# A spectral layer and a gated layer on one core: the forward transform along time over two row groups, and a later start of four inverse tiles

## The chip, the cores and the metric

The kernel runs on one core of one Trainium2 chip. The core has five engines that work side by side, each on its own queue of instructions: TensorE (PE in the profile, with PEld for its weight loads), VectorE (DVE), ScalarE (ACT), GpSimd (POOL) and SyncE (SP), which here issues most transfers. Matrix products land in PSUM, which has eight banks of 128 x 512 numbers of four bytes here; everything else lies in SBUF, and large arrays come from the device's memory by DMA.

The metric is the device time of one execution in microseconds (us), as the median of several runs.

## The reference: what is computed

The input x has 2048 rows (time) of 512 numbers. Four residual layers follow each other; two kinds alternate:

```
x = x + A(layernorm(x));  x = x + B(layernorm(x));  x = x + A(layernorm(x));  x = x + B(layernorm(x))

A(x) = irfft2(rfft2(x) * (w_r + 1j * w_i))          # spectral filter, transform over both axes
B(x) = ((x @ w_gate) * (x @ w_up)) @ w_down         # 512 -> 1792 -> 512, no nonlinearity
```

So each spectral layer is a two-dimensional real Fourier transform, a product with a complex filter of 2048 x 257 numbers, and the inverse transform. Each gated layer is three matrix products. Both layers of a kind use the same weights.

## The kernel before, in words

**Data.** x stays in SBUF all the time as `xs`, 16 tiles of 128 rows by 512. A tile holds 2 x 64 of the 2048 rows. The transform along time is split as 64 points within a tile and 32 across tiles.

**Forward transform** (`fwd_steps`, lines 211 to 283), four steps per tile. `a0`: sums and differences of the halves of a row (fo, fe, on POOL and DVE) and the load of the tile's table `tw`. `a1`: four transposes on TensorE into a bank tp, copied to fs by ACT or DVE; the last argument of `fwd_steps`, `fs_dve`, says for which tiles DVE does it. `a2`: the transform along the 512 features, four matmuls into a bank dp; then dp is scaled by the norm's factor into `us`. dp has real parts (257 columns) and imaginary parts (255 columns) side by side, and rows of two groups of 64; `us` has to put the imaginary parts of a group below its real parts, so four ACT instructions of 64 rows move the four quarters, and POOL clears the two columns that have no imaginary part. `a3`: the transform along time within the tile, for each of two groups one matmul of 128 rows by 257 columns into a bank sp, copied by ACT into E. The steps of one tile stand at steps n, n+1, n+2 and n+4 of a list, so that tiles overlap.

**Middle** (`mid_phase`): transposes, the 32-point transform across tiles, the product with the filter, and back into E.

**Inverse transform** (`inv_steps`, lines 377 to 431). For each tile: `b0` loads its table, `b1` is the transform within the tile (vp, split into a high part vs[0] by ACT and a low part vs[1] by DVE), `b2` the transform along the features (yi, 12 matmuls), `b3` and `b4` add the result to xs, and then come the statistics of the next norm: `stats`, `rstd` and `rest`.

**Preparing the gated layer** (`build_x`, lines 433 to 489). Tiles come in pairs (t, t+4). `norm` makes two normed tiles xn (DVE), `turn` transposes one of them on TensorE into a bank tq, and `forms` makes the sums that the products need: copies into `sx` (ACT), four sums (POOL), and splits into high and low parts: XA (ACT, DVE) and XS (ACT, then POOL). `sx` has one buffer. For the second half of x, `sums` takes the place of `forms`, with a stage tile xf.

**Gated layer** (`unit`, lines 554 to 642). The 1792 hidden features are 14 blocks; a unit is one block with 512 or 256 columns of x. It has seven products (p5, p1, p6, p2, p7, p3, p4; gw, gx, gy, gx, gz, gv, gz in the profile), whose factors on the weights' side are made by ACT and POOL (`forms_w`: wt, rg). Two halves of h follow, split into high and low by ACT and POOL, and the products `down` (db), which DVE adds into xs, are handed on to the next unit.

**Order of the work.** The list of `in_steps` is sorted by step and then by a rank. `weave(main, side, frac)` (line 650) mixes two lists by costs that stand in them: after each entry of the main list, entries of the side list are taken as long as their share of the side's cost is behind the main's share of `frac` times its cost. After entries marked "hold" (the last two products of a unit) none is taken, and what is left comes at the end. While `pin["on"]` is set, each engine keeps the order in which the kernel issues its instructions; outside (forward stage of layer 0, its counterpart at the end of layer 0, middle and first part of the inverse) a scheduler may order them by what is ready.

**Where these lists stand.** In each of two rounds (`layer`): middle; the inverse of the first eight tiles (`o1`: 0, 4, 1, 5, 2, 6, 3, 7), of which the entries below step 9 are issued at once and the rest woven into the units (0, 0) and (1, 0), block 0 and 1 on the first 256 columns; then (0, 1) and (1, 1) on the other 256 columns; then blocks 2 to 12, into which the inverse of the other eight tiles and their `norm`, `turn` and `sums` are woven; then the units of the second half of x. At the end of the first round the forward transform for the second is woven in: tiles 0 to 7 while blocks 11 to 2 run, and 8 to 15 at the last units and after them.

All engine instructions are issued through one helper, so the profile shows line 123 for all of them; groups are told apart by the names of their tiles.

Of the kernel before, what the change touches and what calls it, by code (L numbers as in the profile page):

```python
# [33 lines left out]
def consts():  # L34
    odd = np.arange(1, 256, 2)
    ev2 = np.arange(2, 256, 4)
    ev0 = np.arange(0, 256, 4)
    kd = np.concatenate([ev0, ev2, odd, [256]])
    d2 = np.arange(128)[:, None]
    c, s = _cs(d2 * odd[None], 512)  # L40
    sg = np.where(odd % 4 == 1, 1.0, -1.0)[None]
    fb = np.concatenate([c, -s], 1)
    fe = np.concatenate([-s * sg, -c * sg], 1)
    c, s = _cs(d2 * ev0[None], 512)
    nyq = np.where(d2 % 2 == 0, 1.0, -1.0)
    ui = -s
    ui[:, 0:1] = nyq
    fu = np.concatenate([c, ui], 1)
    c, s = _cs(d2 * ev2[None], 512)
    fv = np.concatenate([c, -s], 1)  # L50
    dfwd = np.concatenate([fb, fe, fu, fv], 1)
    d = np.arange(256)[None]
    blocks = []
    ev = np.concatenate([ev0, ev2])[:, None]
    for ks in (ev, odd[:, None]):
        c, s = _cs(ks * d, 512)
        re, im = 2 * c / 512, -2 * s / 512
# [24 lines left out]
    mid = np.concatenate([f2, g2, np.eye(128)], 1).astype(np.float32)  # L82
    single = lambda a: a.astype(np.float32)
    return dict(kd=kd, dfwd=single(dfwd), dinv=np.stack(_split(dinv), 1), tf=single(m), ti=single(r), mid=mid)


@with_exitstack
def kernel(ctx: ExitStack, tc: tile.TileContext, x, wf, wc, wb, dfwd, dinv, tf, ti, mid, out):
# [7 lines left out]
    XYW = "xyw"  # L96
# [114 lines left out]
    def fwd_steps(get_dc, E, tags, gs, fs_dve):  # L211
# [31 lines left out]
        def a2(t):  # L243
            s, dc = S[t], get_dc()
            fs = s["fs"]
            dp = bank("dp", tags(t)[1])
            dv = dp.rearrange("p (c k) -> p c k", c=2)
            o = 0
            for i, (n, c0) in enumerate(((256, 128), (256, 128), (128, 0), (128, 64))):
                mv = dc[:, o:o + n].rearrange("p (c k) -> p c k", c=2)  # L250
                TE.matmul(dv[:, :, c0:c0 + n // 2], fs[:, 128 * i:128 * i + 128], mv,
                                 start=i == 0, stop=i == 3, skip_group_check=True)
                o += n
            u = s["u"] = temp("us", "g", (128, 2, 257))
            G.memset(u[64:128, :, 0:257:256], 0.0)
            i = nms[t]["ts"].index(t)
            r = nms[t]["r"][:, i:i + 1]
            for jj in range(2):
                q = slice(64 * jj, 64 * jj + 64)
                A.mul(u[0:64, jj, 0:257], dp[q, 0:257], r[q])  # L260
                A.mul(u[64:128, jj, 1:256], dp[q, 257:512], r[q])

        def a3(t):
            s = S[t]
            tw, u = s["tw"], s["u"]
            for jj in range(2):
                sp = bank("sp", tags(t)[2])
                TE.matmul(sp[:, :257], tw[:, jj], u[:, jj, 0:257], start=True, stop=True)
                A.copy(E[:, t, :, jj], sp[:, 0:257])
            s.clear()  # L270

        ops = []
# [101 lines left out]
            if i == 8:  # L374
                dcs["i"] = load_di()

    def inv_steps(E, get_dc, nms, order, tags, build):
        S = [{} for _ in range(16)]

        def b0(t):  # L380
# [38 lines left out]
        ops = []  # L419
        for n, t in enumerate(order):  # L420
            nm = nms[t]
            for d, f, o, c in ((0, b0, 3, 0), (1, b1, 2, 1.0), (2, b2, 4, 1.42), (2, b3, 5, 0.3), (2, b4, 6, 0.3)):
                ops.append((n + d, o, c, lambda f=f, t=t: f(t)))
            ops.append((n + 2, 7, 0.3, lambda t=t: stats(t, nms[t])))
            if t == nm["ts"][-1]:
                ops.append((n + 2, 8, 0, lambda nm=nm: rstd(nm)))
                ops.append((n + 3, 3, 0.1, lambda nm=nm: nm["rest"]()))
            if build and n % 2:
                for k, (c, f) in enumerate(build(nm)):
                    ops.append((n + 4 + k // 2, 9, c, f))  # L430
        return in_steps(ops)

    def build_x(X, nm, tags, stage=None):
# [229 lines left out]
    dcs = {}  # L663
# [8 lines left out]
    for n, o in enumerate(fwd_steps(lambda: dcs["f"], E, lambda t: (XYW[t % 3], "a", "d"), G0, lambda t: t % 2)):  # L672
        o[-1]()
        if n >= 40 and n % 2 and pre:
            for f in pre.pop(0):
                f()
        if n in (30, 38, 46, 54, 62):
            W.load((0, 1, 2, 4, 5)[(n - 30) // 8], E[0:1, n // 8 - 3, 0, 0:1])
    prep_hp(E[0:1, 10, 0, 0:1])

    for layer in range(2):
# [61 lines left out]
        if layer == 0:  # L743
            early = lambda t: "aaa"
            late = lambda t: (XYW[t % 3], "a", "d")
            K = 7
            fb = fwd_steps(lambda: dcs["f"], E, early, [(8, 9), (12, 13)], lambda t: t % 2)
            fc = [(o[0] + K, *o[1:]) for o in fwd_steps(lambda: dcs["f"], E, late, [(10, 11), (14, 15)], lambda t: t % 2)]
            weave(ops, [o for o in fb if o[0] < K])
            W = Filter()  # L750
            for m in range(3):
# [52 lines left out]
```

## Time and profile before

| | us |
|---|---|
| median of 3 runs | 1271.33 |
| lowest, highest run | 1269.25, 1273.46 |
| time of the profiled execution | 1267.3 |
| its span | 1265.5 |
| TensorE busy in it | 1146.9 (91%) |
| POOL busy | 749.7 (59%) |
| DVE busy | 880.9 (70%) |
| ACT busy | 461.6 (36%) |

The page of the profile gives, for one execution, the busy time of each engine, a strip of 40 slices of the span with a digit for each (tenths of the slice that the engine was busy), and groups of instructions as `out<-in` by tile names with a count and a mean time. Answers from the trace add: busy time by windows of time, where after the window's bounds and length come PE, PEld, DVE, ACT and POOL, each with the number of instructions in brackets, then the granted clock of TensorE, the share of the DMA engines and GB/s; the timeline (start, length, engine, instruction, and in square brackets the idle time before it and what ended it); the chain of work that ended last (start, length, engine and tile); and waits (who waited for whom: us in total, times, longest). A row of a tile gives the shortest, median and longest time of one instruction in ns, then the first and last start. Matmuls on fp32 data are recorded as two passes each, so that four matmuls are eight rows.

### The profile page before, as it was taken

The numbers are of one execution on the slowest core, as the hardware profiler recorded it, in microseconds if no ns is written. First come the engines' busy times: TensorE is split into PE (matmuls) and PEld (weight loads), VectorE is DVE, ScalarE is ACT, GpSimd is POOL, SyncE is SP. The second block draws the span as 40 slices with busy tenths as digits, with TensorE's granted clock in tenths as the row PEclk, the third lists the DMA queues.
The fourth block names the chain that finished last, engine by engine and source line by source line (L and its number), as shares of the span: only waits on it lengthen the run. The fifth ranks groups of instructions, "written<-read, shape, count | busy, mean of one in ns | idle before, by whom it ended". The sixth has DMA issues, their size and how long they took to land.

```text
span 1265.5 us, 16593 instructions
## 1 busy us (share of the span) xinstructions
PE 1146.9 (91%) x5804; PEld 943.0 (75%) x5804; DVE 880.9 (70%) x1661; ACT 461.6 (36%) x939; POOL 749.7 (59%) x812
## 2 busy tenths in 40 slices
PE   5889669999998999999988885799998989999998
PEld 4645558888777877888877365688887779788887
DVE  7558756777775887775676886566677767666676
ACT  5776223222233233444326742232232332322221
POOL 4534347666676477775741433576666855877772
PEclk9899889999998999999989997899999999999999
DMA  6532001111210011112105310021110210211111
GB/s 234 196 125 67 20 15 51 51 46 51 67 59 26 1 43 47 46 51 75 42 18 220 113 47 22 1 71 38 50 58 24 79 59 34 67 59 51 34 35 67
DMA packets 30755, 77.68 MB, mean 61 GB/s; under 512 B 3408, under 2 KB 11856, under 8 KB 28368
## 3 DMA queue, kind: packets, MB, share of 16 engines
q1 hardware_dynamic: 29952, 73.54, 17.3%
q0 software_dynamic: 288, 2.10, 0.5%
q8 instruction: 46, 0.75, 0.2%
q10 hardware_dynamic: 432, 0.98, 0.2%
q14 instruction: 37, 0.30, 0.1%
HBM read 72.42 MB, written 4.19 MB: 61 GB/s over the span
## 4 chain that ended last, share of the span: by engine, by line
PE 35%; POOL 14%; issue 6%; DVE 5%; ACT 2%; DMA 1%; POOLq 0%; DVEq 0%; ACTq 0%
PE db L123 11%; PE gz L123 5%; PE gx L123 5%; POOL wt L123 5%; POOL rg L123 3%; PE gw L123 3%; PE gy L123 3%; PE gv L123 3%; POOL h L123 2%; PE dp L123 2%; DVE xs L123 1%; DVE q L123 1%; POOL jz L123 1%; PE sp L123 1%; PE yi L123 1%
## 5 line engine op out<-in xcount | busy, mean ns | idle before, releaser
L123 PE MATMUL db<-wd,h 128*128 128x512 f32 x1344 | 367.5, 399 | 10.2 <-ACT h L123 4.0
L123 DVE TENSOR_TENSOR xs<-xs,db 128x512 f32<-128x512 f32 x448 | 297.0, 681 | 49.0 <-PE db L123 48.8
L123 POOL TENSOR_TENSOR h<-q,h 128x512 fp32r<-128x512 f32 (+1 forms) x144 | 151.6, 1057 | 251.4 <-ACT h L123 169.4
L123 PEld LDWEIGHTS db<-wd,h 128*128 128x128 f32 x1344 | 244.5, 191 | 62.6 <-DVE xs L123 9.3
L123 POOL TENSOR_TENSOR wt<-rg,wt 128x512 fp32r<-128x512 f32 (+1 forms) x216 | 233.8, 1090 | 68.9 <-ACT wt L123 67.4
L123 ACT CAST h<-q 128x512 fp32r<-128x512 f32 (+1 forms) x144 | 75.4, 525 | 330.1 <-DVE q L123 310.8
L123 PE MATMUL gx<-xA,wt 128*128 128x512 f32 (+1 forms) x864 | 185.0, 351 | 2.7 <-ACT s L123 2.7
L123 ACT CAST wt<-rg 128x512 fp32r<-128x512 f32 (+1 forms) x216 | 110.6, 541 | 190.3 <-POOL rg L123 176.2
L123 DVE TENSOR_TENSOR q<-gy,s 128x512 f32<-128x512 f32 (+1 forms) x72 | 41.1, 571 | 177.4 <-ACT wt L123 73.2
L123 PEld LDWEIGHTS gx<-xA,wt 128*128 128x128 f32 x864 | 144.7, 196 | 23.8 <-ACT s L123 4.6
L123 POOL TENSOR_TENSOR rg<-rg 128x256 f32<-128x256 f32 x200 | 149.0, 745 | 10.9
L123 PE MATMUL gw<-xS,wt 128*128 128x512 f32 (+1 forms) x432 | 94.8, 354 | 32.1 <-ACT xS L123 22.2
L123 PEld LDWEIGHTS gw<-xS,wt 128*128 128x128 f32 x432 | 72.4, 196 | 45.2 <-ACT xS L123 23.2
L123 PE MATMUL gy<-xS,wt 128*128 128x512 f32 (+1 forms) x432 | 93.7, 354 | 2.0 <-ACT wt L123 1.4
L123 PE MATMUL gz<-xS,wt 128*128 128x512 f32 (+1 forms) x432 | 90.5, 345 | 0.0
L123 PE MATMUL gv<-xS,wt 128*128 128x512 f32 (+1 forms) x432 | 89.7, 343 | 0.0
L123 PE MATMUL gz<-xA,wt 128*128 128x512 f32 (+1 forms) x432 | 89.0, 341 | 0.0
L123 PEld LDWEIGHTS gy<-xS,wt 128*128 128x128 f32 x432 | 73.0, 199 | 12.0 <-ACT wt L123 1.8
L123 PEld LDWEIGHTS gz<-xS,wt 128*128 128x128 f32 x432 | 72.5, 190 | 12.3
L123 PEld LDWEIGHTS gz<-xA,wt 128*128 128x128 f32 x432 | 72.1, 188 | 12.0
L123 PEld LDWEIGHTS gv<-xS,wt 128*128 128x128 f32 x432 | 71.9, 188 | 12.0
L123 ACT ACTIVATE us<-dp,rs 64x257 f32<-64x257 f32 (+1 forms) x128 | 60.3, 471 | 36.2 <-PE dp L123 29.9
(94 smaller groups left out, 1585.8 us busy)
## 6 DMA issues: line engine op xcount, KB each, us to landing
rg<-in_wb_dram SPq DMA_DIRECT2D x50, 512.0 KB, 3.5
rw<-in_wb_dram SPq DMA_DIRECT2D x52, 256.0 KB, 2.6
wq<-in_wf_dram SPq DMA_DIRECT2D x10, 1024.0 KB, 5.8
wr<-in_wf_dram SPq DMA_DIRECT2D x6, 1024.0 KB, 5.7
tw<-in_tf_dram SPq DMA_DIRECT2D x32, 128.0 KB, 2.4
tw<-in_ti_dram SPq DMA_DIRECT2D x32, 128.0 KB, 2.1
out_dram<-xs SPq DMA_DIRECT2D x16, 256.0 KB, 2.0
xs<-in_x_dram SPq DMA_DIRECT2D x7, 512.0 KB, 7.9
```

Of the source, the lines that this page charges most:

```text
L123: ins = f(*args, **kw)
```

## The change

It has three parts.

1. Forward transform. `us` becomes a plain tile of 128 x 512, written by one scaling of the whole of dp; the clearing on POOL goes. The table `tf` is laid out anew, so that each group of 64 rows of `us` finds its table in the same rows. In `a3` each group's product is two matmuls of 64 rows, over the 257 real and over the 255 imaginary columns, added up in PSUM; the two groups use rows 0 to 63 and 64 to 127, and alternate. Both sp banks are taken before the first matmul. `fs_dve` is false everywhere, so that ACT makes all fs copies.
2. Inverse transform, first eight tiles. Tiles 2, 6, 3 and 7 stand two steps later in the list, with all that follows from them. The weave into the first two units uses 0.95 where it used 0.8.
3. Main weave. The norms of a pair are issued one pair ahead of its transposes.

```diff
-    return dict(..., tf=single(m), ti=single(r), mid=mid)
+    return dict(..., tf=single(m.reshape(2, 64, 16, 2, 128).transpose(3, 1, 2, 0, 4).reshape(128, 32, 128)), ti=single(r), mid=mid)
...
-            u = s["u"] = temp("us", "g", (128, 2, 257))
-            G.memset(u[64:128, :, 0:257:256], 0.0)
+            u = s["u"] = temp("us", "g")
             i = nms[t]["ts"].index(t)
-            r = nms[t]["r"][:, i:i + 1]
-            for jj in range(2):
-                q = slice(64 * jj, 64 * jj + 64)
-                A.mul(u[0:64, jj, 0:257], dp[q, 0:257], r[q])
-                A.mul(u[64:128, jj, 1:256], dp[q, 257:512], r[q])
+            A.mul(u, dp, nms[t]["r"][:, i:i + 1])
 
         def a3(t):
             s = S[t]
             tw, u = s["tw"], s["u"]
+            sp = [bank("sp", tags(t)[2]) for _ in range(2)]
+            for c, (lo, n) in enumerate(((0, 257), (1, 255))):
+                for jj in range(2):
+                    q = slice(64 * jj, 64 * jj + 64)
+                    TE.matmul(sp[jj][:, lo:lo + n], tw[q, c], u[q, 256 * c + lo:256 * c + lo + n],
+                              start=c == 0, stop=c == 1, skip_group_check=True)
             for jj in range(2):
-                sp = bank("sp", tags(t)[2])
-                TE.matmul(sp[:, :257], tw[:, jj], u[:, jj, 0:257], start=True, stop=True)
-                A.copy(E[:, t, :, jj], sp[:, 0:257])
+                A.copy(E[:, t, :, jj], sp[jj][:, 0:257])
...
-    def inv_steps(E, get_dc, nms, order, tags, build):
+    def inv_steps(E, get_dc, nms, order, tags, build, late=()):
...
+            m = n + 2 if t in late else n
             for d, f, o, c in ((0, b0, 3, 0), (1, b1, 2, 1.0), (2, b2, 4, 1.42), (2, b3, 5, 0.3), (2, b4, 6, 0.3)):
-                ops.append((n + d, o, c, lambda f=f, t=t: f(t)))
+                ops.append((m + d, o, c, lambda f=f, t=t: f(t)))
...
-    for n, o in enumerate(fwd_steps(..., lambda t: t % 2)):
+    for n, o in enumerate(fwd_steps(..., lambda t: False)):
...
-                         lambda nm: build_x(X, nm, ("d", "d") if nm["ts"][0] < 2 else ("a", "a")))
+                         lambda nm: build_x(X, nm, ("d", "d") if nm["ts"][0] < 2 else ("a", "a")), (2, 6, 3, 7))
...
-        weave(units([(0, 0), (1, 0)], 0), rest, 0.8)
+        weave(units([(0, 0), (1, 0)], 0), rest, 0.95)
...
-        weave(main, inv2 + [o for pre, _ in both for o in pre], 0.93)
+        pre = [p for p, _ in both]
+        early = [pre[0][0]]
+        for k in range(4):
+            early += [pre[k + 1][0]] if k < 3 else []
+            early += pre[k][1:]
+        weave(main, inv2 + early, 0.93)
...
-            fb = fwd_steps(lambda: dcs["f"], E, early, [(8, 9), (12, 13)], lambda t: t % 2)
+            fb = fwd_steps(lambda: dcs["f"], E, early, [(8, 9), (12, 13)], lambda t: False)
```

The same step m takes the place of n for `stats`, `rstd`, `rest` and the build of a pair, and the list `fc` of the last four forward tiles loses its DVE copies like `fb`.

More of the change, by code (lines that the diff above doesn't have):

```diff
@@ L83, in consts @@
     single = lambda a: a.astype(np.float32)
-    return dict(kd=kd, dfwd=single(dfwd), dinv=np.stack(_split(dinv), 1), tf=single(m), ti=single(r), mid=mid)
+    return dict(kd=kd, dfwd=single(dfwd), dinv=np.stack(_split(dinv), 1), tf=single(m.reshape(2, 64, 16, 2, 128).transpose(3, 1, 2, 0, 4).reshape(128, 32, 128)), ti=single(r), mid=mid)
 @with_exitstack
@@ L421, in inv_steps @@
             nm = nms[t]
+            m = n + 2 if t in late else n
             for d, f, o, c in ((0, b0, 3, 0), (1, b1, 2, 1.0), (2, b2, 4, 1.42), (2, b3, 5, 0.3), (2, b4, 6, 0.3)):
-                ops.append((n + d, o, c, lambda f=f, t=t: f(t)))
-            ops.append((n + 2, 7, 0.3, lambda t=t: stats(t, nms[t])))
+                ops.append((m + d, o, c, lambda f=f, t=t: f(t)))
+            ops.append((m + 2, 7, 0.3, lambda t=t: stats(t, nms[t])))
             if t == nm["ts"][-1]:
-                ops.append((n + 2, 8, 0, lambda nm=nm: rstd(nm)))
-                ops.append((n + 3, 3, 0.1, lambda nm=nm: nm["rest"]()))
+                ops.append((m + 2, 8, 0, lambda nm=nm: rstd(nm)))
+                ops.append((m + 3, 3, 0.1, lambda nm=nm: nm["rest"]()))
             if build and n % 2:
                 for k, (c, f) in enumerate(build(nm)):
-                    ops.append((n + 4 + k // 2, 9, c, f))
+                    ops.append((m + 4 + k // 2, 9, c, f))
         return in_steps(ops)
@@ L671 @@
         pre += [[f[k] for k in g.split()] for g in ("start h0", "h12 l0", "d0", "l12", "d1", "d2", "d3 h34", "h56 l34", "l56 next")]
-    for n, o in enumerate(fwd_steps(lambda: dcs["f"], E, lambda t: (XYW[t % 3], "a", "d"), G0, lambda t: t % 2)):
+    for n, o in enumerate(fwd_steps(lambda: dcs["f"], E, lambda t: (XYW[t % 3], "a", "d"), G0, lambda t: False)):
         o[-1]()
@@ L746 @@
             K = 7
-            fb = fwd_steps(lambda: dcs["f"], E, early, [(8, 9), (12, 13)], lambda t: t % 2)
-            fc = [(o[0] + K, *o[1:]) for o in fwd_steps(lambda: dcs["f"], E, late, [(10, 11), (14, 15)], lambda t: t % 2)]
+            fb = fwd_steps(lambda: dcs["f"], E, early, [(8, 9), (12, 13)], lambda t: False)
+            fc = [(o[0] + K, *o[1:]) for o in fwd_steps(lambda: dcs["f"], E, late, [(10, 11), (14, 15)], lambda t: False)]
             weave(ops, [o for o in fb if o[0] < K])
```

## The prediction

> **What bounds the kernel now.** I read the page first (shares, then the strip of 40 slices), then the busy time by windows of 20 us, then the stretch at each change with windows cut at its own events, and last the waits and the timeline there.
>
> ```profile
> span 1265.5 us, 16593 instructions
> ## 1 busy us (share of the span) xinstructions
> PE 1146.9 (91%) x5804; PEld 943.0 (75%) x5804; DVE 880.9 (70%) x1661; ACT 461.6 (36%) x939; POOL 749.7 (59%) x812
> ...
> PE   5889669999998999999988885799998989999998
> ```
>
> TensorE is 91% busy, so the kernel as a whole is bound by it; but the strip (slices of 31.6 us, counted from 0) has three kinds of places that are not nines: slices 0 to 2 and 20 to 23 (forward transforms and what follows), 4 and 5 with 24 and 25 (inverse transforms and the first units), and the eights of 12, 30 and 32 (end of the main weave and the units behind it). The change works at just these.
>
> ```profile
> core 0: us, PE busy (x) PEld busy (x) DVE busy (x) ACT busy (x) POOL busy (x), PEclk, DMA share, GB/s
> 40.00:60.00 20.00, 14.45 (x79) 12.25 (x78) 9.05 (x23) 16.35 (x39) 11.87 (x17) 0.92 0.35 124
> 600.00:620.00 20.00, 20.00 (x90) 16.56 (x89) 12.42 (x20) 6.74 (x14) 15.51 (x17) 1.00 0.13 40
> 680.00:700.00 20.00, 15.37 (x77) 11.61 (x75) 8.12 (x31) 15.18 (x36) 2.12 (x7) 0.91 0.65 254
> ```
>
> In the forward stages (40 to 60 and 680 to 700) ACT is the busiest engine, with TensorE close behind. Where forward tiles are woven into the gated layer (600 to 620) TensorE is full: every matmul added there is added to the time. The third place, by windows cut at the events of layer 0:
>
> ```profile
> core 0: us, PE busy (x) PEld busy (x) DVE busy (x) ACT busy (x) POOL busy (x), PEclk, DMA share, GB/s
> 140.00:148.20 8.20, 1.52 (x10) 1.11 (x10) 7.98 (x18) 3.55 (x7) 3.59 (x5) 0.84 0.00 1
> 148.20:150.65 2.45, 0.58 (x2) 0.29 (x2) 0.07 (x1) 0.00 (x0) 2.34 (x1) 0.50 0.00 0
> 150.65:173.20 22.55, 18.77 (x123) 17.52 (x123) 12.01 (x28) 4.84 (x10) 6.73 (x7) 0.89 0.09 24
> 173.20:181.44 8.24, 0.61 (x3) 0.29 (x2) 3.13 (x7) 3.50 (x7) 5.60 (x7) 0.69 0.00 0
> ```
>
> From 140 to 181.4 us TensorE loses 8.5 us before the first units, 3.8 us inside them, and 7.6 us before the third unit. No engine is full in the last of these: it is a chain of dependent work.
>
> **The change, part 1: forward transform.** Per tile it removes four ACT scalings of 64 rows, and puts one of 128x512 in their place; removes a small POOL memset; moves twelve copies fs of odd tiles from DVE to ACT; and turns two matmuls of 128 rows by 257 columns into four of 64 rows by 257 or 255 columns.
>
> ```profile
> L123 ACT ACTIVATE us<-dp,rs x128: 457/472/476, 14.5 to 695.5; 64x257 f32<-64x257 f32 x64, 64x255 f32<-64x255 f32 x64
> L123 ACT COPY fs<-tp x20: 567/587/605, 10.9 to 688.4; 128x512 f32<-128x512 f32 x20
> L123 DVE COPY fs<-tp x12: 670/680/692, 13.6 to 689.6; 128x512 f32<-128x512 f32 x12
> L123 PE MATMUL sp<-us,tw x128: 377/380/794, 20.5 to 698.6; 128*128 128x257 f32 x128
> L123 ACT COPY E<-sp x64: 380/391/402, 22.4 to 699.0; 128x257 f32<-128x257 f32 x64
> ```
>
> ACT per tile now: 4 x 0.472 + 2 x 0.391 = 2.67 us, and 0.587 more for even tiles: 2.96 on the mean. After: 0.59 (estimate from the fs copy, same shape and source) + 0.78 + 0.59 = 1.96. ACT gives up 1.0 us per tile, DVE 0.68 on odd tiles.
>
> TensorE per tile, from the chain of layer 1, and the pace at which tiles pass in layer 0 (the second fence, from the timeline: with 44.62 and 47.30 between them, three tiles in 9.07 us, 3.0 us each):
>
> ```profile
> 688.15 0.99 PE sp L123 x4
> 689.14 0.44 PE tp L123 x4
> 689.58 2.62 PE dp L123 x16
> 692.20 0.87 PE sp L123 x4
> 693.07 2.47 issue
> ```
>
> ```profile
> 41.31 1.11 PE L123 MATMUL sp<-us,tw 128*128 128x257 f32 x4 [0.16 <-issue]
> ...
> 50.38 1.11 PE L123 MATMUL sp<-us,tw 128*128 128x257 f32 x4 [0.26 <-issue]
> ```
>
> 0.44 + 1.31 + 0.87 = 2.62 us per tile. Each matmul is recorded as two passes, 0.217 us apart. What four half-height matmuls cost no row shows: the nearest is sp itself. Low end: the halves run side by side at all times, eight passes in the time of four, 0.87 us, nothing added. High end: one after another, 1.74 us. In the order of issue (group 0 twice, group 64 twice, and again) only passes next to each other in different groups can overlap, three pairs of eight passes, which leaves five steps: 1.09 us, +0.22. If TensorE must also run empty between full-height and half-height work, each of two changes per tile shows at most the part of a pass that is hidden today, 0.380 - 0.217 = 0.16. I take +0.35 per tile; ends 0 and 0.87 + 0.33 = +1.2. The accumulation also lets the first E copy start only after the third matmul, some 0.5 us later; two banks are free for it, so nothing waits.
>
> The Trainium skill, TensorEngine Tiling (Array Packing), Key Properties, says that different tiles execute in parallel but that a change of tiling mode drains TensorE. No run here shows either. By the first clause alone part 1 would be free on TensorE in the woven tiles; by the second the two changes per tile come on top, and the rival without overlap below is what is left if the first does not hold for this order of issue.
>
> Layer 0's forward stage: the pace goes from 3.0 (ACT) to 2.62 + 0.35 = 2.97 (TensorE), so the pace gains nothing. What can be gained are stalls in which ACT was late:
>
> ```profile
> PE sp L123 <- ACT E L123: 5.7, 2, 4.7
> ```
>
> That is a 4.7 us wait for an E copy that stood on ACT behind casts of weights, themselves waiting for POOL; the lighter ACT does not remove POOL's lateness, so I count a third, and 1.3 us (4 x 0.47 less 0.59) on the last tile: -3. Ends: -10 (both stalls and a pace of 2.62 over ten tiles) and +6 (pace 3.8 on some of them). Layer 1: eight tiles woven where TensorE is full, 8 x 0.35 = +2.8; ends 0 and 9.6. The last eight tiles, 660 to 700: -2.6 from the scalings on the path at two places (the wait of 2.47 above is one), +1.6 for the half of the added 2.8 that is on the path: -1; ends -5 and +6. The memsets (32 of 0.1 us) and the other layout of the same table cost nothing: POOL is idle beside them, the transfers keep their size.
>
> **Part 2: inverse tiles moved into the first units.** Inverse tiles 2, 6, 3, 7 are due two steps later, so of eight tiles five are complete before the first product (0, 4, 1, 5, 2), and two vp stages and three yi stages stand in the woven list, where one yi stood. Working the list through with its own costs (main 4.76 + 7.48, times 0.95; side 10.88) gives the order on TensorE's queue, which is written as it is issued: the transpose of the second tile of pair (2, 6), and both of (3, 7), come behind the last product of unit (1, 0). In the kernel before, the one of (2, 6) stands behind that unit's third product, with four products left to cover it.
>
> ```profile
> 138.32 2.37 POOL L123 TENSOR_TENSOR xS<-sx,xS 128x1024 fp32r<-128x1024 f32 x1 [1.16 <-ACT xS L123]
> 142.24 0.63 PE L123 MATMUL tq<-midt,xn 128*128 128x128 f32 x4 [0.32 <-DVE xn L123]
> 150.65 1.44 PE L123 MATMUL gw<-xS,wt 128*128 128x256 f32 x5 [1.83 <-POOL xS L123]
> 165.27 0.60 PE L123 MATMUL tq<-midt,xn 128*128 128x128 f32 x4
> 171.11 2.39 POOL L123 TENSOR_TENSOR xS<-sx,xS 128x1024 fp32r<-128x1024 f32 x1 [1.16 <-ACT xS L123]
> 174.75 3.14 POOL L123 TENSOR_TENSOR sx<-sx 128x256 f32<-128x256 f32 x4 [1.25 <-ACT sx L123]
> 179.04 2.34 POOL L123 TENSOR_TENSOR xS<-sx,xS 128x1024 fp32r<-128x1024 f32 x1 [1.16 <-ACT xS L123]
> 181.44 1.44 PE L123 MATMUL gw<-xS,wt 128*128 128x256 f32 x5 [1.84 <-POOL xS L123]
> ```
>
> and from the chain of layer 1, one vp stage and one yi stage:
>
> ```profile
> 743.46 0.96 PE vp L123 x8
> 872.83 1.41 PE yi L123 x12
> ```
>
> From the end of that transpose (165.87) to the third unit's product (181.44) are 15.6 us: copies, POOL sums, cast, POOL low part of (2, 6), then the same for (3, 7), because tile sx has one buffer. Today TensorE works through the first 7.3 us of it. After the change it has two transposes to do.
>
> The sum for a layer. The first units start earlier: transposes of (1, 5) no longer queue behind two tiles' work, and the earliest start is then sx free (140.69 today, some 1.5 earlier) plus one copy-sums-cast-low run, about 8.1 (142.87 to 150.65, and 0.3 for gaps): 147.6 for 150.65, -3. The woven part gains 2 vp and 2 yi, 2 x 0.96 + 2 x 1.41 = 4.7, loses three transposes of 0.44, and closes some of its 3.8 us of waits, I take 2.5: 22.55 + 4.7 - 1.3 - 2.5 = 23.5, ending at 171.1. Then 0.44 + 15.6 and 1 us for ACT's casts of h that stand ahead of the copies: 188.1 against 181.4, **+7 per layer**. Ends: +10 (no wait closes); -3 (the pair's chain starts as early as today, and only the earlier start is left). SP: the twiddle load of tile 7 moves into the units, two products ahead of its use; hidden. Two layers: +14.
>
> **Part 3: norms one pair ahead.** In the main weave the order becomes norm of the next pair, then both transposes and sums of this one.
>
> ```profile
> PE tq L123 <- DVE xn L123: 5.4, 3, 2.6
> ```
>
> ```profile
> 990.00:1000.00 10.00, 8.97 (x49) 7.46 (x48) 8.41 (x13) 2.46 (x4) 8.98 (x11) 1.00 0.27 87
> ```
>
> Between 940 and 1045 us TensorE waits 5.4 us in three waits for xn, and as long in layer 0. The last two should go wholly; the first pair's norm is only one entry ahead. But POOL, 90% busy in these slices (8.98 of 10 us, the fifth engine), is next late with sums and weights, so I count half: -2.5 per layer, ends 0 and -5.4; -5 for two. Four xn and one rw fill the five buffers of their pool; a late rw would be the price, covered today by a unit of some 13 us.
>
> **Sum.** -3 + 2.8 - 1 + 14 - 5 = +7.8. The profiled execution took 1267.3, 4 us under the median of the three runs shown (1271.33) and just below the lowest: 1275 by its own time, 1279 by the median.
>
> **The rivals.** Slower still: *the halves do not overlap*. +1.2 per tile instead of 0.35: woven tiles +6.8, layer 0's pace 2.62 + 1.2 = 3.8 over ten tiles +8, the tail +5: about 1299. For it: nothing in this trace ever overlaps two matmuls beyond the fill of a pass. Against: halves touch different rows and different banks.
>
> Faster: *the handover is cheaper than I count*. The turning point is where the last transpose of (2, 6) ends: if under 166 us the third unit starts no later than today. It needs the two moved tiles to fit wholly into TensorE's waits of 8.5 + 3.8 us ahead of it. Then part 2 is -3 per layer, and the sum -3 + 2.8 - 1 - 6 - 5 = -12: 1259. For it: 20 us idle per layer in this stretch. Against: the order of the queue.
>
> No change that can be told: *ACT's relief is worth its high end*, -10 and -5 in the two unwoven forward stages, 11 less than I took: 1268.
>
> **How the numbers follow.** A measurement of this kernel tells about 0.3%, 3.8 us, from no change. Stalled handover with overlap 0.48 (own range 1275 to 1290), no overlap 0.14, handover helps 0.24, relief balances 0.14. Slower 0.62, same 0.14, faster 0.24. Range 1258 to 1297: from the helping handover to the case without overlap, leaving out about 2 in 10.
>
> **What would show it.** Right: a TensorE gap of some 15 us before the third unit, ended by POOL xS, and first products 3 us earlier; sp groups of eight passes with 1.1 to 1.4 us each; ACT near 10 of 20 in 40 to 60; waits for xn gone after 960. Wrong: a gap under 9 us there; sp at 0.9 or 1.7 us; a forward stage of layer 0 shorter by more than 8 us, which would mean that ACT's order, not its load, made the stalls.

## The result, and the profile after

The changed kernel takes 1292.86 us (median of four runs, 1291.91 to 1295.83); the kernel before, beside it on the same chip, 1271.40. The ratio is 1.0173, with a 95% interval of 1.0149 to 1.0197: 1.7% slower. The profiled execution has a span of 1291.4 us, 25.9 more than that of before; the medians differ by 21.5, since the profiled execution of before (1267.3) was 4 us faster than its median. First the page of the changed kernel, its head, TensorE's row and the strip of slices:

```profile
span 1291.4 us, 16692 instructions
## 1 busy us (share of the span) xinstructions
PE 1163.6 (90%) x5932; PEld 949.3 (74%) x5932; DVE 867.8 (67%) x1649; ACT 427.1 (33%) x855; POOL 746.6 (58%) x780
...
PE   6888549999989999999989875599999999999998
```

TensorE is busy 16.7 us longer, of which 128 more passes of sp are a part, but that is not 25.9. The hollows at slices 4 and 5 and at 24 and 25 are still there. The kernel's own time between its landmarks shows where the difference lies. The landmarks are starts on TensorE in the timelines: the first vp of the inverse, the third unit's products (gw, five rows), the db behind the last wait of the main weave, the first late tp of the forward transform, the first zp of the middle of layer 1.

| stretch | before, us | after, us | measured | predicted |
|---|---|---|---|---|
| start to first vp, layer 0 (forward, middle) | 114.31 | 111.61 | -2.7 | -3 |
| first vp to third unit, layer 0 (part 2) | 67.13 | 78.79 | +11.7 | +7 |
| third unit to end of main weave, layer 0 (part 3) | 213.81 | 213.72 | -0.1 | -2.5 |
| on to the last eight forward tiles (woven tiles) | 262.81 | 266.08 | +3.3 | +2.8 |
| the last eight forward tiles | 42.14 | 41.54 | -0.6 | -1 |
| middle, layer 1 | 36.27 | 37.61 | +1.3 | 0 |
| first vp to third unit, layer 1 (part 2) | 66.89 | 79.30 | +12.4 | +7 |
| third unit to end of main weave, layer 1 (part 3) | 211.99 | 212.28 | +0.3 | -2.5 |
| the rest | 250.15 | 250.47 | +0.3 | 0 |

The two rows of part 2 hold 24.1 of the 25.9 us. The change doesn't touch the middle; that of layer 1 is 1.3 us longer, with a granted clock of TensorE of 0.50 in its first 3.3 us (711.74 to 715.03), where the one of before had 1.00 throughout. The windows of the changed kernel that answer to those shown of before, cut at its own events: the idle stretch ahead of the first units, their low part, the woven part up to the end of the transposes of (2, 6), and the chain to the third unit.

```profile
core 0: us, PE busy (x) PEld busy (x) DVE busy (x) ACT busy (x) POOL busy (x), PEclk, DMA share, GB/s
135.00:142.89 7.89, 0.00 (x0) 0.00 (x0) 3.13 (x7) 3.37 (x7) 5.24 (x5) 0.50 0.00 0
142.89:145.35 2.46, 0.58 (x2) 0.29 (x2) 0.00 (x0) 0.00 (x0) 2.34 (x1) 0.50 0.00 0
145.35:173.64 28.29, 23.42 (x155) 21.97 (x155) 17.53 (x44) 3.63 (x9) 2.29 (x3) 0.89 0.09 29
173.64:190.40 16.76, 2.54 (x10) 1.73 (x10) 3.81 (x8) 6.06 (x11) 11.36 (x11) 0.56 0.00 0
```

The first units start at 145.35 instead of 150.65. Then the woven part takes 28.29 us instead of 22.55, and TensorE still waits 4.87 us inside it, more than the 3.78 of before. Behind it stand 16.76 us in which TensorE works 2.54: the gap has doubled from 8.24. Its timeline (start, length, engine, instruction, and in brackets the idle time before it and what ended it):

```profile
145.35 1.43 PE L123 MATMUL gw<-xS,wt 128*128 128x256 f32 x5 [1.84 <-POOL xS L123]
...
155.95 0.98 PE L123 MATMUL gw<-xS,wt 128*128 128x256 f32 x6 [1.66 <-DVE q L123]
...
168.89 1.09 PE L123 MATMUL tq<-midt,xn 128*128 128x128 f32 x4 [3.20 <-DVE xn L123]
...
173.04 0.60 PE L123 MATMUL tq<-midt,xn 128*128 128x128 f32 x4
...
175.67 3.30 POOL L123 TENSOR_TENSOR sx<-sx 128x256 f32<-128x256 f32 x4 [0.32 <-ACT sx L123]
...
177.67 1.96 PE L123 MATMUL tq<-midt,xn 128*128 128x128 f32 x8 [4.04 <-DVE xn L123]
...
180.13 2.34 POOL L123 TENSOR_TENSOR xS<-sx,xS 128x1024 fp32r<-128x1024 f32 x1 [1.16 <-ACT xS L123]
...
183.72 3.13 POOL L123 TENSOR_TENSOR sx<-sx 128x256 f32<-128x256 f32 x4 [1.25 <-ACT sx L123]
...
187.98 0.58 PE L123 MATMUL gw<-xS,wt 128*128 128x256 f32 x1 [8.35 <-ACT xS L123]
...
190.40 1.43 PE L123 MATMUL gw<-xS,wt 128*128 128x256 f32 x5 [1.84 <-POOL xS L123]
```

The waits are those of a handover that is on time nowhere. The products of a unit wait for q, because VectorE has the late tiles' additions ahead of it; the transposes of (2, 6) wait for xn, the last link of the late tiles' norm; those of (3, 7) wait again. From 173.04 on nothing is left to cover POOL's two rounds of sums and low part.

The forward stage of layer 0, and the stretch where forward tiles are woven in:

```profile
core 0: us, PE busy (x) PEld busy (x) DVE busy (x) ACT busy (x) POOL busy (x), PEclk, DMA share, GB/s
40.00:60.00 20.00, 16.52 (x96) 12.76 (x96) 8.87 (x15) 10.71 (x24) 11.06 (x13) 0.91 0.50 179
600.00:620.00 20.00, 20.00 (x97) 15.71 (x96) 10.33 (x17) 6.10 (x13) 11.26 (x11) 1.00 0.20 64
```

ACT falls from 16.35 to 10.71 of 20 us, as it should, and TensorE rises from 14.45 to 16.52: the relief was taken up by the other engine. The pace of the tiles there, in the timeline:

```profile
36.07 1.14 PE L123 MATMUL sp<-us,tw 64*128 64x257 f32 x8
37.14 0.44 PE L123 MATMUL tp<-midt,fo 128*128 128x128 f32 x2
...
39.03 1.14 PE L123 MATMUL sp<-us,tw 64*128 64x257 f32 x8
```

Eight passes of half height take 1.14 us as a group, where four of full height took 1.11; each pass is as long as before (0.377). So the two row groups do run side by side. In the trace the eight passes start as four pairs, at 36.070 and 36.077, 36.391 and 36.398, 36.608 and 36.614, 36.827 and 36.834: 7 ns apart within a pair, 0.22 to 0.32 us between pairs. The pace is 2.96 us (39.03 less 36.07), forecast at 2.97.

### The profile page after: what moved, and what is told of

The parts are those of the page before. It is cut to its first block, busy times and chain, and to the rows that moved or that the text cites. A ratio compares the mean times of both kernels' runs of the same rounds, so it can differ in the third digit from the quotient of the medians.

```text
span 1291.4 us, 16692 instructions
## 1 busy us (share of the span) xinstructions
PE 1163.6 (90%) x5932; PEld 949.3 (74%) x5932; DVE 867.8 (67%) x1649; ACT 427.1 (33%) x855; POOL 746.6 (58%) x780
## 4 chain that ended last, share of the span: by engine, by line
PE 33%; POOL 16%; issue 7%; DVE 6%; ACT 2%; DMA 0%; POOLq 0%; DVEq 0%; ACTq 0%
PE db L123 10%; POOL wt L123 5%; PE gz L123 5%; PE gx L123 5%; POOL rg L123 3%; PE gw L123 3%; PE gv L123 2%; PE gy L123 2%; POOL h L123 2%; DVE xs L123 2%; DVE q L123 2%; PE dp L123 1%; PE sp L123 1%; POOL wd L123 1%; PE yi L123 1%
## 5 line engine op out<-in xcount | busy, mean ns | idle before, releaser
L123 POOL TENSOR_TENSOR wd<-rw,wd 128x512 fp32r<-128x512 f32 x52 | 67.3, 1296 | 6.4 <-ACT wd L123 6.4
```

Source lines behind the costliest of these rows:

```text
L123: ins = f(*args, **kw)
```

## The experiments

**Each part alone.** Four kernels were run on one chip beside the kernel before.

e1_undo_late is the changed kernel with part 2 taken out:

```diff
-                         lambda nm: build_x(...), (2, 6, 3, 7))
+                         lambda nm: build_x(...))
...
-        weave(units([(0, 0), (1, 0)], 0), rest, 0.95)
+        weave(units([(0, 0), (1, 0)], 0), rest, 0.8)
```

> The changed kernel with part 2 undone (no late tiles, 0.8). Theory A, the handover carries the whole loss: the trace after puts +9.9 us on layer 0 and +13.8 us on layer 1 between the start of the middle and the third unit, so this kernel comes to 1267 to 1271, within 0.3% of before. Rival B, part of the loss is the forward transform's extra passes in the woven tiles and the norms' order pressing on POOL: it stays at 1275 to 1283. Third unit's first product at about 180.5 us (181.4 before less the 0.9 us that the forward stage is shorter) by A.

Measured 1268.31 us, ratio to before 0.9988 (0.9966 to 1.0010). The whole loss is gone with part 2. The first units and the third in its timeline:

```profile
148.16 1.43 PE L123 MATMUL gw<-xS,wt 128*128 128x256 f32 x5 [1.84 <-POOL xS L123]
...
178.81 1.44 PE L123 MATMUL gw<-xS,wt 128*128 128x256 f32 x5 [1.84 <-POOL xS L123]
```

They are 30.65 us apart, as before (30.79), and 45.05 in the changed kernel.

e2_late_only is the kernel before with part 2 and nothing else:

```diff
+            m = n + 2 if t in late else n
...
+                         lambda nm: build_x(...), (2, 6, 3, 7))
...
+        weave(units([(0, 0), (1, 0)], 0), rest, 0.95)
```

> The kernel before with part 2 alone. Theory A: +22 to +25 us, 1293 to 1296, with waits of TensorE of 8 us before the third unit's first product in each layer. Rival B: +10 to +15, the rest coming from the other parts' meeting with it.

Measured 1292.71 us, ratio 1.0186 (1.0150 to 1.0222): part 2 alone is as slow as the whole change. Its third unit:

```profile
170.83 0.63 PE L123 MATMUL tq<-midt,xn 128*128 128x128 f32 x4 [3.23 <-DVE xn L123]
...
179.58 1.96 PE L123 MATMUL tq<-midt,xn 128*128 128x128 f32 x8 [4.04 <-DVE xn L123]
...
192.31 1.43 PE L123 MATMUL gw<-xS,wt 128*128 128x256 f32 x5 [1.84 <-POOL xS L123]
```

The same two waits for xn, 3.23 and 4.04, stand here without any change to the forward transform or to the main weave.

e3_forward_only is the kernel before with part 1 (the diff of part 1, above):

```diff
+            u = s["u"] = temp("us", "g")
...
+            A.mul(u, dp, nms[t]["r"][:, i:i + 1])
```

> The kernel before with part 1 alone. By the milestones of the trace after: -0.9 us in layer 0's forward stage, +3 to +4 where eight tiles are woven into a full TensorE, -0.6 in the last eight tiles: +1 to +3 us, not to be told from before at 2% and hardly at 0.3%. Rival: the unwoven stages gain more once nothing else is changed, -3 to -6 us.

Measured 1270.14 us, ratio 0.9997 (0.9979 to 1.0015): no difference. In its trace the first vp is 2.6 us earlier (111.68 for 114.31; 0.9 of it in the forward stage, whose end, the first zp, comes at 75.46 for 76.34), and the stretch with the woven tiles 4.5 longer (267.3 for 262.8).

e4_norm_only is the kernel before with part 3:

```diff
+        early = [pre[0][0]]
+        for k in range(4):
+            early += [pre[k + 1][0]] if k < 3 else []
+            early += pre[k][1:]
+        weave(main, inv2 + early, 0.93)
```

> The kernel before with part 3 alone. Theory: POOL takes over, the 5.4 us of waits for xn per layer go and come back as a wait for the weights' low parts (POOL wt) of about 2.7 us and slower work behind: 0 to -2 us in all. Rival, as predicted before: half of the waits is kept, -5 us.

Measured 1262.69 us, ratio 0.9941 (0.9921 to 0.9962): the only part that gains by itself, and more than either expectation. Of the waits for xn of 5.4 us in each layer 1.4 are left, and another one is there, seen in the view of the waits, 320 to 405 us:

```profile
PE gw L123 <- POOL wt L123: 2.7, 1, 2.7
```

POOL's weights are what is late next. Of the 9.1 us between the medians (1271.80 and 1262.69) the traces show 3.3, the difference of the spans: 2.0 of it between the third unit and the end of the main weave in layer 0 (211.85 for 213.81) and 0.4 in layer 1. The other 5.8 are the distance of the two profiled executions from their medians, before 4.5 under it and e4 1.3 above; what makes executions of one kernel differ by that much stays open.

**Is it the share of the weave or the late tiles?** e5_late_frac08 is the changed kernel with the old share:

```diff
-        weave(units([(0, 0), (1, 0)], 0), rest, 0.95)
+        weave(units([(0, 0), (1, 0)], 0), rest, 0.8)
```

> The changed kernel with the late tiles kept and the weave's 0.95 set back to 0.8. By the list's costs the last transpose of pair (2, 6) then stands ahead of the last three products of unit (1, 0) instead of behind them, and those of (3, 7) ahead of the last two. Theory A, the loss is the chain of two builds behind the last transpose of (2, 6) (16.8 us in the trace after) left uncovered by its place in the queue: each layer gets 5 to 8 us back, 1277 to 1283. Rival B, the loss is the moved work itself: 1288 to 1294.

Measured 1277.47 us, ratio 1.0058 (1.0036 to 1.0081), inside the range of Theory A. The order of TensorE's products in its trace is the expected one: the last transposes of (2, 6) stand ahead of the last three products of unit (1, 0), those of (3, 7) ahead of the last two. About 15 of the 24.5 us that part 2 costs in this kernel (1292.86 less 1268.31) came from spreading the woven list over 95% of the two units, which puts the last pair's transposes behind their last product; about 9 from the late tiles themselves. Place in the queue is the larger cause, and not the only one.

**One late tile in place of four.** e6_one_late is the kernel before with part 3, with tile 7 alone late, and with the woven list drawn forward:

```diff
-                         lambda nm: build_x(...))
+                         lambda nm: build_x(...), (7,))
...
-        weave(units([(0, 0), (1, 0)], 0), rest, 0.8)
+        weave(units([(0, 0), (1, 0)], 0), rest, 0.6)
```

> The kernel before with part 3, inverse tile 7 alone late, and the weave at 0.6, so that pair (2, 6) is transposed right behind the first product and its chain runs under the units. Theory A: the third unit starts about 5 us earlier than before in each layer: 1250 to 1256 against 1262.7 with part 3 alone. Rival B: the transposes stall TensorE's queue on xn ahead of the products, and nothing is won: 1261 to 1266.

Measured 1249.14 us, ratio 0.9852 (0.9816 to 0.9888): it beats both kernels. Its handover:

```profile
149.61 1.44 PE L123 MATMUL gw<-xS,wt 128*128 128x256 f32 x5 [1.84 <-POOL xS L123]
...
166.16 0.66 PE L123 MATMUL tq<-midt,xn 128*128 128x128 f32 x4 [2.78 <-DVE xn L123]
...
173.53 2.36 POOL L123 TENSOR_TENSOR xS<-sx,xS 128x1024 fp32r<-128x1024 f32 x1 [1.16 <-ACT xS L123]
...
175.95 0.86 PE L123 MATMUL gw<-xS,wt 128*128 128x256 f32 x5 [1.38 <-POOL xS L123]
...
178.79 0.87 PE L123 MATMUL gx<-xA,wt 128*128 128x256 f32 x6
```

Here the transposes of (3, 7) stand ahead of the last four products of unit (1, 0), and these cover POOL's round; the third unit waits 1.38 us. The five products cost 0.86 us instead of 1.43. The two windows below, of the changed kernel and of this one, hold the same five groups of products (gw, gx, gy, db, gx) behind the handover:

```profile
190.40:196.51 6.11, 6.11 (x27) 5.82 (x27) 1.54 (x3) 0.37 (x1) 0.00 (x0) 0.53 0.01 3
```

```profile
175.95:179.50 3.55, 3.55 (x27) 3.42 (x28) 1.26 (x4) 0.78 (x2) 1.52 (x2) 1.00 0.00 0
```

With a granted clock of 0.53 they take 6.11 us, with 1.00 they take 3.55. So the idle stretch here costs 2.6 us more after it has ended. The clock fell inside the wait of 4.04 us ahead of 177.67: it was 1.00 from 172.31 to 175.72, and 0.50 from 175.72, through the wait of 8.35, until 196.20, after 5.8 us of products. The Trainium skill, "TensorE: Matmul & The Clock Gate", Part 1 (The HAM clock gate), says that TensorE's clock is halved once it has been idle for a window of some 3.4 us and comes back only after a busy one; these traces agree that it is halved in long waits, but show it after shorter ones too. The same wait in the main weave, first in the changed kernel, then in e1_undo_late:

```profile
356.55 1.04 PE L123 MATMUL tq<-midt,xn 128*128 128x128 f32 x4 [1.36 <-DVE xn L123]
```

```profile
344.75 0.63 PE L123 MATMUL tq<-midt,xn 128*128 128x128 f32 x4 [1.36 <-DVE xn L123]
```

Behind it the granted clock was 0.50 in the one (356.63 to 360.04) and 1.00 in the other. So the length of one wait doesn't settle the clock, and the 1.38 us of e6 can't be called short enough.

Against e4_norm_only, e6's first vp to third unit is 4.5 us shorter in layer 0 (62.79 for 67.27) and 4.0 in layer 1 (62.80 for 66.83), and third unit to end of weave 2.5 and 1.8 (209.38 for 211.85, 209.78 for 211.56), the clock behind the gap in the main. These make 12.8 of the 15.6 us between the two spans.

**Which of the two edits did it?** e10_weave06 is part 3 with the share at 0.6 and no late tile:

```diff
-        weave(units([(0, 0), (1, 0)], 0), rest, 0.8)
+        weave(units([(0, 0), (1, 0)], 0), rest, 0.6)
```

> Part 3 alone, with the weave into the first two units at 0.6 in place of 0.8 and no inverse tile later. Theory A: the gain of the version with tile 7 alone later (1249.1) comes from one tile's work leaving the stretch ahead of the first units, so that the weave at 0.6 by itself leaves the third unit where it was: 1259 to 1266 (part 3 alone: 1262.7), wait ahead of the third unit 6 to 9 us. Rival B: an earlier place of the last pair in the queue is all of it, whichever tile is late: 1247 to 1253, wait ahead of the third unit under 2 us.

Measured 1262.64 us, ratio 0.9936 (0.9913 to 0.9959), as part 3 alone (1262.69). The time is Theory A's, but the wait is not the 6 to 9 us it expected:

```profile
169.02 1.09 PE L123 MATMUL tq<-midt,xn 128*128 128x128 f32 x4 [2.25 <-DVE xn L123]
...
171.19 1.05 PE L123 MATMUL tq<-midt,xn 128*128 128x128 f32 x4
...
181.86 1.42 PE L123 MATMUL gw<-xS,wt 128*128 128x256 f32 x5 [2.03 <-POOL xS L123]
```

The gap is nearly closed (2.03 us), and yet the third unit starts where that of e4 does (182.03). The transposes of (3, 7) were only drawn ahead of products, which are held up with them by the wait for xn. What then runs late, at a granted clock of 0.55 (160.00 to 173.11, for 1.00 in e4), fills what was idle; POOL's sums behind them start no sooner (175.12 for 175.34). The length of a gap is no measure here; the start of the last pair's chain is.

To move that it takes the late tile, but not by a shorter stretch ahead of the first units, as Theory A has it: from the first vp to the first units it is 36.45 us in e6 and 36.32 in e10. What changes is the list. In e10 the norm of (2, 6) stands behind tile 7's products yi and additions; in e6 it stands ahead of them, and VectorE makes it before the first units. The first transposes of (2, 6) inside the units, first e6, then e10:

```profile
150.85 1.05 PE L123 MATMUL tq<-midt,xn 128*128 128x128 f32 x4
```

```profile
162.27 1.94 PE L123 MATMUL tq<-midt,xn 128*128 128x128 f32 x8 [1.91 <-DVE xn L123]
```

So POOL starts its round for (2, 6) at 157.03 in e6 and at 167.02 in e10, and is free for that of (3, 7), which starts at 169.18 and 175.12.

e11_after_late7 makes the same edit to the changed kernel itself, with its row groups:

```diff
-                         lambda nm: build_x(...), (2, 6, 3, 7))
+                         lambda nm: build_x(...), (7,))
...
-        weave(units([(0, 0), (1, 0)], 0), rest, 0.95)
+        weave(units([(0, 0), (1, 0)], 0), rest, 0.6)
```

> The changed kernel (parts 1 and 3 whole) with only tile 7 later and the weave at 0.6. Theory A: the parts add up; the loss of 24 us is the place of the last two pairs and nothing else in the changed kernel stands against the gain: 1268.3 (parts 1 and 3) less the 13.5 that this edit won on part 3 alone, 1252 to 1258. Rival B: with the row groups in place the stretch ahead of the first units is no longer what it was, and the edit wins little: 1263 or more.

Measured 1255.49 us, ratio 0.9899 (0.9833 to 0.9965), inside the range of Theory A. Its third unit:

```profile
173.64 0.86 PE L123 MATMUL gw<-xS,wt 128*128 128x256 f32 x5 [1.49 <-POOL xS L123]
```

Four late tiles turn a gap of 8 us into one of 17; one turns it into 1.5, in both kernels.

**What the halves do.** e7_groups_in_turn is part 1 alone with the matmuls issued group by group, real and imaginary of rows 0 to 63 first:

```diff
-            for c, (lo, n) in enumerate(((0, 257), (1, 255))):
-                for jj in range(2):
+            for jj in range(2):
+                for c, (lo, n) in enumerate(((0, 257), (1, 255))):
```

> Part 1 alone, with both matmuls of rows 0 to 63 issued ahead of both of rows 64 to 127. In the trace after, the eight passes of a tile start in four pairs, 7 ns apart within a pair and 0.217 us between pairs, though the matmuls are issued one after another. Theory A, only neighbours in the queue go side by side: now one pair at most, seven or eight starts, 1.3 to 1.6 us from the first pass to the last in place of 0.76. Rival B, each half of the rows has a queue of its own: still four pairs, 0.76 us.

Measured 1270.04 us in one run. The passes still start as four pairs, 13 to 14 ns apart (38.228 and 38.242, 38.549 and 38.562, 38.766 and 38.779, 38.985 and 38.998), and a tile's group is as long as with the other order:

```profile
38.23 1.14 PE L123 MATMUL sp<-us,tw 64*128 64x257 f32 x8
39.30 0.44 PE L123 MATMUL tp<-midt,fo 128*128 128x128 f32 x2
```

In the forward stage of layer 0 a scheduler may reorder the matmuls; in the woven tiles, where each engine keeps the order of issue, the passes pair in the same way (538.518 and 538.532, 538.839 and 538.852, and so on). The prediction's count, that only neighbours in the order of issue overlap, falls: the overlap is whole in either order.

Then where does the added time per tile come from? From the start of the last product before sp to the start of the first product behind it, a tile of before takes 0.98 us beside dp and tp and 0.91 or 1.10 beside the gated layer's products; in the changed kernel 1.27 and 1.38 to 1.39. e12_full_between puts one full-height transpose between the two pairs of half-height matmuls, e13_full_behind puts it behind both:

```diff
+                if c == 0:
+                    TE.transpose(sp[0][:, 384:512], u[:, 0:128], ident)
```

```diff
+            TE.transpose(sp[0][:, 384:512], u[:, 0:128], ident)
```

> Part 1 alone, with one transpose of 128 by 128 added per forward tile, between the real and the imaginary pair of half-height matmuls; it writes columns of the bank that nobody reads, so that the output is the same. Own time of a transpose from the rows of tp (0.44 for four): 0.11. Theory A (each change between full-height and half-height work makes TensorE run empty, which is the whole price of part 1): two changes more per tile, so that from the first pass of sp to the next product beside dp and tp it is 1.27 + 0.11 + 0.29 to 0.47 = 1.67 to 1.85 us. Rival B (the price belongs to half-height matmuls themselves, not to the changes): 1.27 + 0.11 = 1.38.

> The same added transpose, but behind all four half-height matmuls, so that it adds work and no change of height. Both theories: 1.27 + 0.11 = 1.38 us from the first pass of sp to the next product beside dp and tp, and about 1271 to 1274 as a whole; it is what the one before is held against. If this one is as long as that one, the place makes no difference and Theory A falls.

In e12 the added transpose falls into the middle of a running sum in its bank, so that the sums of group 0 are not those of the reference, other than its expectation says; the instructions timed are the same in number and shape. One run each: 1294.32 us for e12, 1280.85 for e13. First e12, then e13:

```profile
39.64 0.70 PE L123 MATMUL sp<-us,tw 64*128 64x257 f32 x4
40.28 0.33 PE L123 MATMUL sp<-midt,us 128*128 128x128 f32 x1
40.54 0.70 PE L123 MATMUL sp<-us,tw 64*128 64x255 f32 x4
41.17 0.44 PE L123 MATMUL tp<-midt,fo 128*128 128x128 f32 x2
...
43.06 0.70 PE L123 MATMUL sp<-us,tw 64*128 64x257 f32 x4
```

```profile
37.62 1.14 PE L123 MATMUL sp<-us,tw 64*128 64x257 f32 x8
38.68 0.33 PE L123 MATMUL sp<-midt,us 128*128 128x128 f32 x1
38.85 0.38 PE L123 MATMUL tp<-midt,fo 128*128 128x128 f32 x2
...
40.69 1.14 PE L123 MATMUL sp<-us,tw 64*128 64x257 f32 x8
```

From sp to tp it is 1.53 us with the transpose between (41.17 less 39.64) and 1.23 with it behind (38.85 less 37.62): 0.30 for two changes of height, the same as part 1 itself pays for two (1.27 less 0.98). Measured as the expectations have it, with the step into sp, it is 1.73 and 1.44 beside dp and tp, and in the woven tiles 1.84 and 1.47 to 1.55. The place decides: the price is that of the change, not of half-height work. The pace of the tiles says the same, 3.42 us (43.06 less 39.64) against 3.07. As a whole e13 took 7 us more than the 1274 that stood as its upper end; its first zp comes 6.1 us later than in e3 (81.52 for 75.46), with waits of 4.5 and 4.7 us ahead of sp in two places, so that an added transpose in this stage costs more than its own time; why, these runs don't show.

The Trainium skill, "TensorEngine Tiling (Array Packing)", Key Properties, said both: that different tiles execute in parallel, and that a change of tiling mode drains TensorE. These runs agree with the first, by the 7 ns between the passes of a pair; the 0.29 us for two changes fit the second, though no run shows the draining itself.

**Row groups only where nothing is woven.** e8_rows_unwoven is part 3 with the new form of part 1 for the tiles of layer 0 and the last ones, and the old form for the eight woven tiles:

```diff
+        def fwd_steps(get_dc, E, tags, gs, rows):
...
+            s["tw"] = twiddle(tg if rows else tf, t)
...
+            if rows:
+                u = s["u"] = temp("us", "g")
```

> The kernel before with part 3, and part 1 in the unwoven forward stages only (layer 0's, and the last eight tiles), with both layouts of the table. Theory A, part 1 loses where TensorE is full (3 to 8 us in the traces) and wins a little where ACT is the busiest: 1258 to 1261 against 1262.7 with part 3 alone. Rival B, the unwoven stages win nothing by it: 1262 to 1265.

Measured 1262.96 us, ratio 0.9951 (0.9929 to 0.9973), against 1262.69 without any row groups: what the unwoven stages win can't be told from nothing. With the woven tiles too it is 1268.31 (e1). So on top of part 3 the woven tiles cost some 5 us, for 3.2 by the rows (five of 0.47 and three of 0.29). The traces show a longer woven stretch in each pair: 4.5 us in e1 against e8 (270.4 for 265.9), 4.5 in e3 against before, 3.3 in the changed kernel. But the time of e3 as a whole does not show it; this difference stays open.

## Why the prediction was right or wrong

Slower was forecast for a reason that holds: the late tiles move the last transposes behind the last product, and a chain of POOL's work stands uncovered. What failed is its size: +7.8 us was forecast, 1279, and 1292.86 was measured, 21.5 more than before. The term to blame is part 2, +14 in the sum and 24.1 in the traces: 10.1 of the 18.1 us by which the two spans differ from the sum (25.9 against 7.8) are part 2, 5.2 are part 3.

**Part 2, the term that failed: the woven part of 23.5 us.** The prediction had it at 22.55 + 4.7 - 1.3 - 2.5. Up to the start of the last transposes of (2, 6) it measured 27.7 (145.35 to 173.04). The term of -2.5, that new work would close waits, had the wrong sign: in place of two waits for xn (2.41 and 1.37) there are one for q (1.66) and one for xn (3.20), since the tiles moved into the units bring not just TensorE's work but a chain through VectorE (additions, statistics, norm), which shares that engine with the gate's own factors. TensorE's idle time in this part rose from 3.78 to 4.87. That is 3.6 of the 4.2 us missed in this part (layer 1 is alike: 27.71 from the first units to those transposes); the rest is busy time, 22.8 up to them for 18.77, more than the 3.4 counted. The earlier start was -2.6 and -2.4 for -3 (first vp to first units: 33.74 for 36.34, 34.23 for 36.64). The chain behind the transposes was 17.4 (173.04 to 190.40) for 17.0: right in size. Its cause was put too simply as "because tile sx has one buffer": POOL is busy 11.36 us of the 16.76, and the buffer shows only in the 1.25 us ahead of 183.72 in which POOL waits for ACT's copies. A second buffer was not tried.

**The gap's after-effect was not in the sum**, nor needed to be, since the gap of before had it too; but it is why e6 and e11 also gain in the stretch behind the third unit.

**Part 3: -5 forecast, nothing seen.** Alone it gains 0.6%. Inside the changed kernel the third unit to the end of the weave is as long as before (213.72 for 213.81), though of the 5.4 us of waits for xn only 1.4 are left, near the forecast; with part 2 undone (e1) it is 211.89. The step "POOL is next late, so I count half" named the right engine: the wait for wt of 2.7 us stands there in both. The 2 us that are lost beside part 2 in layer 0 are the granted clock in the main: 0.4 in the products right behind the third unit, and 1.3 behind the wait for xn at 356.55, shown above, where e1 ran at full clock. That is one execution of each, and need not repeat.

**Part 1: near in sum, wrong in reasoning.** +0.35 per tile was taken; 0.29 to 0.47 measured, the pace 2.96 for 2.97, the woven stretch +3.3 for +2.8, the tail -0.6 for -1. But 0.22 of the 0.35 was to come from passes that don't overlap, and 0.16 from each change at most. The overlap is whole (e7), and the changes carry all of it (e12 against e13). Two errors met in one sum, and that it came out near is luck. So is layer 0's -2.7 for -3: the first zp is only 0.9 us earlier (75.41 for 76.34). TensorE's waits for an E copy, of which a third was to go, rose from 5.7 to 7.5 us in the forward stage. The other 1.8 us lie in the middle, which the change leaves as it is: TensorE ran there at a clock of 0.50 for 3.4 us in the trace of before (90.92 to 94.33), and at 1.00 throughout in that of the changed kernel. The scaling of 128 x 512 took 0.687 us, for 0.59 from the fs copy.

The rival in which the halves don't overlap is excluded by the pairs, the one in which the handover is cheap by the last transposes of (2, 6), which end at 173.64 and not under 166; and ACT's relief did not balance anything: the forward stage of layer 0 is 0.9 us shorter, not 10. That ACT would be near 10 of 20 us there was right, 10.71.

## What to carry to other kernels

When work is moved into a stretch to cover a wait, follow the moved work's whole chain through every engine's queue to its last consumer: it covers only if its consumers still stand ahead of the products that are meant to hide them. Move one piece first, not four; here one late tile gained 13 us, with part 3 under it, and four lost 24. And splitting a matmul into row groups pays for each change between full-height and half-height work, so four of them between full-height ones gained nothing here; a longer run of them between two changes was not tried.

## What the runs showed of the hardware that was not expected

Passes of two row groups start 7 ns apart when the groups alternate, and 13 to 14 ns apart when all of one group is issued before the other: in this trace TensorE pairs matmuls of different row groups that are not next to each other. Two changes between full-height and half-height fp32 work, in and out, cost 0.29 us beside dp and tp and 0.29 to 0.47 beside the gated layer's products. At a granted clock of 0.53 products took 6.11 us that take 3.55 at full clock. After the same wait of 1.36 us the clock was 0.50 in one trace and 1.00 in another, and inside the two spans the stretches at 0.50 last 3.4 us or a multiple of it (3.4, 6.8, 10.2, 13.7, 20.5). Two traces can so differ by 1 to 2 us in a stretch that the change doesn't touch, as the two middles show.
